# A decode-attention kernel: the feed-forward and most of the output projection in column tiles, and its code moved by a block

## The chip, the cores and the metric

The kernel runs on one core of one Trainium2 chip. The metric is the device time of one execution in microseconds (us), as the median of several runs. The profile shows one execution with the work of each engine: PE is TensorE (PEld its weight loads, issued ahead of their matmuls), DVE is VectorE, ACT is ScalarE, POOL is GpSimd, and SP is SyncE, which issues nearly all transfers here.

## What is computed

One decode step of attention over a long cache, plus a small feed-forward net, on the same normalized input (2 sequences, one new token each, width 512, 32 heads of 128, 8192 cached keys and values per head, feed-forward width 1792, all in bf16):

```python
def _A_ref(x, k_cache, v_cache, wq, wo):
    q = (x @ wq).reshape(B, Sq, H, Dh).transpose(0, 2, 1, 3)
    scores = jnp.einsum("bhqd,bhkd->bhqk", q, k_cache) * (Dh ** -0.5)
    p = softmax(scores, axis=-1)
    o = jnp.einsum("bhqk,bhkd->bhqd", p, v_cache)
    return o.transpose(0, 2, 1, 3).reshape(B, Sq, H * Dh) @ wo

def _B_ref(x, w1, w2):
    return jnp.maximum(x @ w1, 0) @ w2

xn = layernorm(x)
out = x + _A_ref(xn, k_cache, v_cache, wq, wo) + _B_ref(xn, w1, w2)
```

The caches are 134 MB each; everything else together is 12 MB.

## The kernel before, in words

**Tiling.** The 64 pairs of sequence and head are taken four at a time, in 16 steps. In a step each of the 128 partitions holds 256 keys of one pair (32 partitions per pair), so one K tile `ks` is 128 x 32768 bf16, 8.4 MB, and one V tile `vs` the same. Each exists once: a tile is loaded again only when its last reader is done.

**A step on TensorE** (the loop over `n16`). It waits for K (`dK[0]`, and `dK[1]` for the second half where a load is cut in two). Line 275 transposes 256 blocks of 128x128 into PSUM (`tp`); VectorE and ScalarE copy them to `kT` (line 429). Line 282 multiplies each by the four queries into `Sc`, the scores. VectorE takes maxima (476, 483), TensorE turns and spreads them (294, 300), ScalarE makes the exponentials `prm` (550). Line 335 multiplies the 256 blocks of V by `prm` into `ot`. Then, in all but the last two steps, line 346 issues `WARM` = 24 matmuls of 512 columns whose result nobody reads. All this is written out in code, some 1,600 instructions of a weight load and a matmul each per pair, and the loop jumps back over them.

**Transfers** are queued by SP in program order (line 182): K of the next step when the transposes of this one are done (`pT`), V of the next when line 335 is done (`sW`). The loads of steps 0 and 15 (K) and of steps 1 and 15 (V) are cut in halves. After the last transposes SP issues `w1`, `w2` and `wo` into the place of `ks` (lines 190 to 194), `wo` in four pieces cut at rows 18, 26 and 30 of 32 (`cuts`).

**Ahead of the loop**: `wq` into the place of `vs`, the layer norm on VectorE, four transposes (248), the q projection in 32 matmuls of 512 columns (254), four transposes (264). **Behind the loop** on TensorE, in its order: the softmax denominators (356, four f32 matmuls), the residual x into `fin` (362), the hidden layer (373: 14 x 4 matmuls with 128x128 weights and 2 moving columns, read from `w1` with a step of 14 elements), the transposes of the heads' outputs (385), their spreading over partitions (389), then line 400 in `project`: `w2` (14 x 4 matmuls) and the four pieces of `wo` (32 x 4), each again with 128x128 weights and 2 moving columns, all accumulated in `fin`, which is transposed with the features on the partitions. At last VectorE copies `fin` to `yT` (526), TensorE transposes it (420), VectorE copies it to `osb` (528) and SP stores it.

Of the kernel before, what the change touches and what calls it, by code (L numbers as in the profile page):

```python
# [7 lines left out]
ALU = mybir.AluOpType  # L8
ACTF = mybir.ActivationFunctionType
AX = mybir.AxisListType  # L10

U = 4
# [4 lines left out]
TR = (21, 25)  # L17
BC = 32
WARM = 24
ON_ACT = (0, 3, 5)  # L20


@with_exitstack
def kernel(
# [13 lines left out]
    P = 128  # L38
    HP = P // U
    bf16 = mybir.dt.bfloat16  # L40
    f32 = mybir.dt.float32

    Bsz, Sq, D = A_x.shape
# [3 lines left out]
    KT = D // P  # L47
    FJ = Dff // P
    KB = Sk // HP
    N = Bsz * H  # L50
    NP = N // U
    WJ = H * Dh // P
# [7 lines left out]
    QG = H * Dh // 512  # L60
    QH = 512 // Dh
    Z = (QG - 1) * Bsz

    inv_sqrt = float(Dh) ** -0.5
    eps = 1e-5
# [3 lines left out]
    def sb(shape, dt, name):  # L69
        return ctx.enter_context(nc.sbuf_tensor(name, shape, dt))  # L70
# [4 lines left out]
    def sem(name):  # L75
# [6 lines left out]
    wo_sb = ks[:, 0:WJ * D].rearrange("p (j n) -> p j n", j=WJ)  # L82
    w1_sb = ks[:, WJ * D:WJ * D + KT * Dff].rearrange("p (kt f) -> p kt f", kt=KT)
    w2_sb = ks[:, WJ * D + KT * Dff:WJ * D + KT * Dff + FJ * D].rearrange(
        "p (j n) -> p j n", j=FJ
    )
    kT = [sb([P, EG, P], bf16, f"kT{i}") for i in range(NG)]
    identb = sb([P, P], bf16, "identb")
# [8 lines left out]
    rinv = sb([Bsz, 1], f32, "rinv")  # L97
    xn = sb([Bsz, KT, P], bf16, "xn")

    xz = sb([P, KT, 2 * Z + Bsz], bf16, "xz")  # L100
    qs = sb([QG * Bsz, 512], bf16, "qs")
    qb = sb([P, N], bf16, "qb")
    q4 = sb([P, U], bf16, "q4")
# [15 lines left out]
    OG = sb([P, 2, N], f32, "OG")  # L119
    OTn = sb([P, Bsz, H], bf16, "OTn")  # L120
    Ob = sb([H, Bsz, Dh], bf16, "Ob")
    OX = sb([P, WJ, Bsz], bf16, "OX")
    hT = sb([P, FJ, Bsz], bf16, "hT")
    yT = sb([P, Bsz, KT], bf16, "yT")
    osb = sb([Bsz * KT, P], bf16, "osb")

# [25 lines left out]
    wo_v = A_wo.rearrange("(p j) n -> p j n", j=WJ)  # L152
    cuts = (0, 18, 26, 30, WJ)
    NC = len(cuts) - 1

    KSPLIT = (0, NP - 1)
    VSPLIT = (1, NP - 1)
# [4 lines left out]
    tpx = tp[0][:].rearrange("p g k -> p (g k)")[:, 0:KT * Bsz].rearrange(  # L162
        "p (kt b) -> p kt b", b=Bsz
    )
    hp = ms[:, 128:128 + FJ * Bsz].rearrange("p (j b) -> p j b", b=Bsz)
    ox = ms[:, 256:256 + Bsz * WJ]
    fin = Sc[:, 512:512 + KT * Bsz]

# [42 lines left out]
    @(lambda f: f(nc.gpsimd))  # L211
    def _(g):
        g.memset(identb[:], 0.0).then_inc(sG, 1)
        g.memset(sel[:], 0.0).then_inc(sG, 1)
        g.memset(onesh[:], 0.0).then_inc(sG, 1)
        g.wait_ge(sG, 1)
        g.affine_select(
            out=identb[:], in_=identb[:], compare_op=ALU.not_equal, fill=1.0,
            base=0, pattern=[[-1, P]], channel_multiplier=1,
        ).then_inc(sI, 1)  # L220
        g.wait_ge(sG, 2)
        g.affine_select(
            out=sel[:], in_=sel[:], compare_op=ALU.not_equal, fill=1.0,
            base=0, pattern=[[-1, DQ], [1, P]], channel_multiplier=-DQ,
        ).then_inc(sI, 1)
        g.wait_ge(sI, 2)
        g.memset(prm[:], 0.0).then_inc(sG, 1)
        g.wait_ge(sG, 4)
        for u in range(U):
            g.memset(onesh[u * HP:(u + 1) * HP, u, :], 1.0).then_inc(sI, 1)  # L230
            g.wait_ge(sI, 3 + u)
        g.wait_ge(sV, 100)
        for t in range(NP):
            if t > 0:
                g.wait_ge(sS, 2 * t)
            g.tensor_copy(q4[:], qb[:, U * t:U * t + U]).then_inc(sQ1, 1)  # L236
            for d, split in ((dK, KSPLIT), (dV, VSPLIT)):
                if t not in split:
                    g.wait_ge(d[0], 16 * (t + 1)).then_inc(d[1], 16)
        g.wait_ge(dO, 16).then_inc(sG, 1)  # L240


    @(lambda f: f(nc.tensor))
    def _(pe):
        pe.wait_ge(sI, 1)
        pe.wait_ge(sV, 5)
        for kt in range(KT):
            i = pe.transpose(tpx[:, kt, :], xn[:, kt, :], identb[0:Bsz, 0:Bsz])
        i.then_inc(sQ, 1)
        pe.wait_ge(sV, 6)  # L250
        pe.wait_ge(dQ, 16)
        for g in range(QG):
# [53 lines left out]
        with pe.Fori(16, NL + 1, 16) as n16:  # L306
            pe.wait_ge(dK[0], n16)
            for e in range(NG):
                if e == NG // 2:
                    pe.wait_ge(dK[1], n16)  # L310
                if e >= 4:
                    pe.wait_ge(kR[(e - 4) % HG], h[(e - 4) // HG])
                transposes(e)
                if e >= LAG:
                    scores(e - LAG)
            pe.wait_ge(sQ1, reg)
            for e in range(NG - LAG, NG):
                if e >= NG - 4:
                    pe.wait_ge(kR[e % HG], h[e // HG])
                scores(e)  # L320
                if e == TR[0]:
                    turn(0)
                if e == TR[1]:
                    spread(0)
            pe.wait_ge(sO, reg)
            for kk in range(KB):
                i, first = divmod(kk, KB // 2)
                if first == 0:
                    pe.wait_ge(sP, g[i])
                    if i == 0:  # L330
                        turn(1)
                    pe.wait_ge(dV[i], n16)
                if kk == BC:
                    spread(1)
                t = pe.matmul(  # L335
                    oh[:, i, :],
                    lhsT=vs[:, kk * Dh:(kk + 1) * Dh],
                    rhs=rep(prm[:, kk, :], REP),
                    start=(first == 0),
                    stop=(first == KB // 2 - 1),  # L340
                )
                if first == KB // 2 - 1:
                    t.then_inc(sW, 1)
            with pe.If_lt(reg, NP - 1):
                for i in range(WARM):
                    pe.matmul(  # L346
                        ms[:], lhsT=identb[:],
                        rhs=identb[:].rearrange("p (o k) -> p o k", o=1).to_broadcast([P, 4, P]),
                        start=True, stop=True,
                    )  # L350
            advance(pe, regs)

        pe.wait_ge(sI, 2 + U)
# [4 lines left out]
                start=True, stop=True,  # L358
            )
        t.then_inc(sH, 1)  # L360
        for k in range(KT):
            pe.matmul(
                fin[:, k * Bsz:(k + 1) * Bsz],
                lhsT=xsb[:, k * P:(k + 1) * P],
                rhs=identb[0:Bsz, 0:Bsz],
                start=(k == 0),
                stop=False,
            )
        pe.wait_ge(dW1, 16)
        w1_v = w1_sb.rearrange("p kt (f j) -> p kt j f", j=FJ)  # L370
        for j in range(FJ):
            for kt in range(KT):
                i = pe.matmul(
                    hp[:, j, :],
                    lhsT=w1_v[:, kt, j, :],
                    rhs=xz[:, kt, Z:Z + Bsz],
                    start=(kt == 0),
                    stop=(kt == KT - 1),
                )
        i.then_inc(sF, 1)  # L380

        pe.wait_ge(sV, 108)
        tO = tp[0][0:H, 0:Bsz, :]
        for b in range(Bsz):
            t = pe.transpose(tO[:, b, :], OTn[:, b, :], identb[:])
        t.then_inc(sH, 1)
        pe.wait_ge(sV, 109)
        for dq in range(DQ):
            t = pe.matmul(
# [5 lines left out]
            )  # L395
        t.then_inc(sH, 1)

        def project(w, j, x, last=False):
            for k in range(KT):
                t = pe.matmul(  # L400
                    fin[:, k * Bsz:(k + 1) * Bsz],
                    lhsT=w[:, j, k * P:(k + 1) * P],
                    rhs=x[:, j, :],
                    start=False,
                    stop=(last and k == KT - 1),
                )
            return t

        pe.wait_ge(sF, 2)
        pe.wait_ge(dW2, 16)  # L410
        for j in range(FJ):
            project(w2_sb, j, hT)
        pe.wait_ge(sV, 110)
        for c in range(NC):
            pe.wait_ge(*piece[c])
            for j in range(cuts[c], cuts[c + 1]):
                t = project(wo_sb, j, OX, j == WJ - 1)
        t.then_inc(sH, 1)
        pe.wait_ge(sV, 111)
        pe.transpose(  # L420
            tp[1][0:Bsz * KT, 0, :], yT[:].rearrange("p b c -> p (b c)"), identb[:]
        ).then_inc(sH, 1)

    def kcopies(eng, act, h):
# [8 lines left out]
    def _(v):  # L433
        v.memset(eps_t[:], eps).then_inc(sV, 1)
        v.memset(onesb[:], 1.0)
        v.memset(xz[:], 0.0).then_inc(sZ, 1)
        v.wait_ge(dX, 16)
        v.bn_stats(out=stats[:], in_=xsb[:]).then_inc(sV, 1)
        v.wait_ge(sV, 2)
# [50 lines left out]
        def both(ap):  # L490
# [21 lines left out]
        v.tensor_tensor(  # L512
            out=OTn[:].rearrange("p b h -> p (b h)"), in0=OG[:, 0, :], in1=OG[:, 1, :], op=ALU.add
        ).then_inc(sV, 1)
        v.wait_ge(sF, 1)
        v.tensor_scalar(
            out=hT[:], in0=hp, scalar1=0.0, scalar2=None, op0=ALU.max,
        ).then_inc(sF, 1)
        v.wait_ge(sH, 2)
        v.tensor_copy(Ob[:], tp[0][0:H, 0:Bsz, :]).then_inc(sV, 1)  # L520
        v.wait_ge(sH, 3)
        v.tensor_copy(
            OX[:], ox.rearrange("p (b j) -> p j b", b=Bsz)
        ).then_inc(sV, 1)
        v.wait_ge(sH, 4)
        v.tensor_copy(yT[:], fin.rearrange("p (c b) -> p b c", c=KT)).then_inc(sV, 1)
        v.wait_ge(sH, 5)
        v.tensor_copy(osb[:], tp[1][0:Bsz * KT, 0, :]).then_inc(sE, 1)


    @(lambda f: f(nc.scalar))
    def _(a):
# [29 lines left out]
            advance(a, regs)  # L562
        a.wait_ge(sV, 102)
        a.activation(out=F[:], in_=df[:], func=ACTF.Exp, scale=1.0).then_inc(sA, 1)
# [1 line left out]
_INS = ['A_x', 'A_k_cache', 'A_v_cache', 'A_wq', 'A_wo', 'B_x', 'B_w1', 'B_w2']  # L566
_OUTS = [((2, 1, 512), 'bfloat16')]
# [25 lines left out]
```

## Time and profile before

| | |
|---|---|
| median of 5 runs | 659.32 us (658.63 to 660.49) |
| the profiled execution, its own time | 659.06 us |
| its span in the profile | 657.2 us |
| busy share of the span: PE, PEld, DVE, ACT, POOL | 90%, 82%, 40%, 44%, 1% |
| moved from memory | 280.5 MB, 427 GB/s over the span |
| granted TensorE clock, mean | 0.98 |

The span is what the profile covers; 1.86 us of the execution's time lie around it. Lines of the chain give start, length, and the engine and line, or the transfer, that the time went to; "issue" is time in which the engine waited for nothing that the profile shows. Lines of the timeline give start, length, engine, line, operation and count, and in brackets the idle time ahead of it with what ended it. Matmul ends are modelled, so their starts are the better guide.

### The profile page before, as it was taken

How to read it: one execution, taken by the hardware profiler on the slowest of the kernel's cores; microseconds unless marked ns; L12 is line 12 of the kernel's file. 1: busy time of each engine (PE TensorE's matmuls, PEld its weight loads, DVE VectorE, ACT ScalarE, POOL GpSimd, SP SyncE). 2: the span in 40 equal slices, each digit the busy share in tenths (PEclk: the TensorE clock that was granted, in tenths of full speed). 3: DMA queues.
4: the chain of work that ended last, by engine and by line, in shares of the span. 5: the costliest groups of instructions: out<-in, count | busy, mean ns of one | idle time of the engine just before them, and what ended most of it. 6: DMA issues, size and time to landing. Idle time of an engine off the chain costs nothing.

```text
span 657.2 us, 27600 instructions
## 1 busy us (share of the span) xinstructions
PE 592.9 (90%) x12987; PEld 535.8 (82%) x12987; DVE 261.7 (40%) x503; ACT 290.7 (44%) x532; POOL 7.1 (1%) x30
## 2 busy tenths in 40 slices
PE   2786999999999999999989999998999999999997
PEld 0586887978878797887969888796987879698986
DVE  1440451717235071633507153260715426071721
ACT  1332543536344363634526354353735435372820
POOL 2000000000000000000000000000000000000000
PEclk9986999999999999999999999999999999999996
DMA  9999999999999999999999999999999999999996
GB/s 383 444 441 425 408 431 443 443 419 447 415 447 431 431 443 419 443 431 435 431 427 443 431 439 423 435 439 427 447 423 435 439 427 447 419 435 417 435 420 271
DMA packets 6223, 280.66 MB, mean 427 GB/s; under 512 B 706, under 2 KB 708, under 8 KB 964
## 3 DMA queue, kind: packets, MB, share of 16 engines
q1 hardware_dynamic: 6208, 280.50, 98.9%
q8 instruction: 8, 0.13, 0.1%
q14 instruction: 3, 0.02, 0.0%
q10 hardware_dynamic: 4, 0.00, 0.0%
HBM read 280.50 MB, written 0.00 MB: 427 GB/s over the span
## 4 chain that ended last, share of the span: by engine, by line
DMA 57%; PE 41%; issue 1%; DVE 0%; SPq 0%; ACT 0%; ACTq 0%
DMA ks<-in_A_k_cache_dram 53%; PE tp L275 34%; DMA ks<-in_A_wo_dram 4%; PE Sc L282 3%; PE ot L335 3%; PE ms L346 1%; DVE mcol L476 0%; ACT L429 0%; ACT kT L429 0%; PE Sc L400 0%; SPq L194 0%; PE ms L294 0%; PE ms L300 0%; SPq L191 0%; SPq L182 0%
## 5 line engine op out<-in xcount | busy, mean ns | idle before, releaser
L429 DVE COPY kT<-tp 128x1024 bf16<-128x1024 bf16 x320 | 209.2, 687 | 248.2 <-PE tp L275 242.5
L275 PEld LDWEIGHTS tp<-identb,ks 128*128 128x128 bf16 x4096 | 230.1, 98 | 26.6 <-DMA ks<-in_A_k_cache_dram 25.2
L275 PE MATMUL tp<-identb,ks 128*128 128x128 bf16 x4096 | 233.1, 220 | 19.4 <-DMA ks<-in_A_k_cache_dram 18.5
L429 ACT COPY kT<-tp 128x1024 bf16<-128x1024 bf16 x192 | 188.1, 1014 | 130.5 <-PE tp L275 130.5
L282 PE MATMUL Sc<-q,kT 128*128 128x64 bf16 (+8 forms) x4096 | 134.2, 192 | 3.2 <-issue 3.1
L282 PEld LDWEIGHTS Sc<-q,kT 128*128 128x128 bf16 x4096 | 129.6, 98 | 4.7 <-issue 3.4
L335 PE MATMUL ot<-prm,vs 128*128 128x64 bf16 x4096 | 130.6, 192 | 1.6 <-issue 1.6
L335 PEld LDWEIGHTS ot<-prm,vs 128*128 128x128 bf16 x4096 | 126.6, 97 | 3.5 <-issue 1.7
L346 PE MATMUL ms<-identb 128*128 128x512 bf16 x336 | 74.8, 379 | 0.0
L476 DVE TENSOR_REDUCE mcol<-Sc 32x1 bf16<-32x128 f32 x128 | 37.0, 289 | 93.6 <-PE Sc L282 92.3
L550 ACT ACTIVATE prm<-Sc,nm 32x128 bf16<-32x128 f32 x128 | 68.9, 538 | 5.4
L545 ACT COPY nm<-ms 128x4 f32<-128x4 f32 x32 | 5.2, 162 | 139.9 <-PE ms L300 139.9
L346 PEld LDWEIGHTS ms<-identb 128*128 128x128 bf16 x336 | 31.9, 98 | 36.4
L561 ACT COPY OTf<-ot 128x8 f32 x16 | 2.6, 165 | 69.9 <-PE ot L335 69.9
L550 ACT ACTIVATION_READ_ACCUMULATOR prm<-Sc,nm x128 | 32.0, 250 | 0.0
L294 PE MATMUL ms<-identb,mcol 128*1 128x128 bf16 x32 | 7.0, 218 | 22.1 <-DVE mcol L476 22.1
L429 ACT ACT_TABLE_LOAD x16 | 20.5, 1283 | 3.7 <-issue 3.6
L294 PEld LDWEIGHTS ms<-identb,mcol 128*1 128x1 bf16 x32 | 2.5, 79 | 23.9 <-issue 23.1
L254 PE MATMUL ot<-vs,xz 128*16 128x512 bf16 x32 | 8.5, 431 | 8.6 <-DMA vs<-in_A_wq_dram 8.6
L483 DVE TENSOR_REDUCE mx<-ms 1x4 bf16<-1x128 bf16 x32 | 8.9, 279 | 13.8 <-PE ms L294 13.8
L254 PEld LDWEIGHTS ot<-vs,xz 128*16 128x16 bf16 x32 | 3.1, 98 | 13.6 <-issue 10.7
L236 POOL COPY q<-qb 128x4 bf16<-128x4 bf16 x16 | 3.0, 186 | 590.8 <-PE Sc L282 572.5
(61 smaller groups left out, 47.6 us busy)
## 6 DMA issues: line engine op xcount, KB each, us to landing
ks<-in_A_k_cache_dram SPq DMA_DIRECT2D x4, 4096.0 KB, 23.0
vs<-in_A_v_cache_dram SPq DMA_DIRECT2D x4, 4096.0 KB, 21.8
vs<-in_A_wq_dram SPq DMA_DIRECT2D x1, 4096.0 KB, 12.1
ks<-in_B_w_dram SPq DMA_DIRECT2D x2, 1792.0 KB, 16.5
ks<-in_A_wo_dram SPq DMA_DIRECT2D x1, 2304.0 KB
ks<-in_A_wo_dram SPq DMA_DIRECT2D x1, 1024.0 KB, 26.4
ks<-in_A_wo_dram SPq DMA_DIRECT2D x1, 512.0 KB, 27.1
ks<-in_A_wo_dram SPq DMA_DIRECT2D x1, 256.0 KB, 27.3
```

What stands on the lines that cost most here:

```text
L236: g.tensor_copy(q4[:], qb[:, U * t:U * t + U]).then_inc(sQ1, 1)
L254: i = pe.matmul(qp, lhsT=xz[:, kt, Z - g * Bsz:Z - g * Bsz + QG * Bsz], rhs=vs[:, (kt * QG + g) * 512:(kt * QG + g + 1) * 512], start=(g = ...
L275: t = pe.transpose(tp[e % 4][:, i, :], ks[:, kk * Dh:(kk + 1) * Dh], identb[:])
L282: t = pe.matmul(Sc[:, U * kk:U * (kk + n)], lhsT=kT[e][:, i, :], rhs=rep(q4[:], n), start=True, stop=True,)
L294: pe.transpose(trp[:, i * P:(i + 1) * P], mcol[:, i:i + 1], identb[:]).then_inc(sT, 1)
L335: t = pe.matmul(oh[:, i, :], lhsT=vs[:, kk * Dh:(kk + 1) * Dh], rhs=rep(prm[:, kk, :], REP), start=(first == 0), stop=(first == KB // 2 - 1),)
L346: pe.matmul(ms[:], lhsT=identb[:], rhs=identb[:].rearrange("p (o k) -> p o k", o=1).to_broadcast([P, 4, P]), start=True, stop=True,)
L429: fn(kT[e][:], tp[e % 4][:]).then_inc(kR[e % HG], 1)
L476: m = v.tensor_reduce(out=mcol[own, i:i + 1], in_=S[own, i * KB // 2:(i + 1) * KB // 2, u], axis=AX.X, op=ALU.max,)
L483: v.tensor_reduce(out=mx[:, i, :], in_=trp[:, i * P:(i + 1) * P].rearrange("o (u m) -> o u m", u=U), axis=AX.X, op=ALU.max, negate=True,). ...
L545: a.copy(nm[:, i, :], bc[:, i, :]).then_inc(sN, 1)
L550: x = a.activation(out=prm[own, k, u], in_=S[own, k, u], func=ACTF.Exp, bias=nm[own, i, u:u + 1], scale=1.0, accum_out=RS[own, i, bass.ds( ...
```

## The change

The order of the transfers and the arithmetic stay. Five things change.

1. **The hidden layer** swaps its operands: the stationary operand is the input, padded with zeros to `CT` = 32 columns, and the moving one is 512 columns of `w1`. Four matmuls in turn write the four groups of 32 partitions of one PSUM bank (`tile(hp, c)`). ScalarE copies the bank to SBUF as bf16 (`hb`), TensorE transposes it (four transposes), VectorE applies the maximum into `hT`, whose unused columns GpSimd has set to zero.
2. **`w2` and pieces 0 and 1 of `wo`** are taken the same way, 14 + 18 + 8 matmuls of 512 columns, spread by `j % 4` over four groups of 32 partitions of `y`; x is added with one more. VectorE copies `y` to SBUF as f32 (`ys`), and four f32 matmuls with `sel2`, a matrix of ones and zeros that adds the four groups, bring it into `fin`. Pieces 2 and 3 stay as they were; the four f32 matmuls stand between them.
3. **51 matmuls** of 128x128 that nobody reads (`EARLY`) stand behind the first four transposes.
4. **The 24 unused matmuls** of a step become a loop of 4 times 6, and step one skips them too.
5. `sel2` is made by VectorE ahead of the layer norm; two areas are cleared by GpSimd.

```diff
+EARLY = 51
+CT = 32
+    TC = P // CT
+    QW = 512 // P
+    first_j = [min(c * QW, FJ - QW) for c in range(TC)]
+    slots = sorted({j - f + c * QW: j for c, f in enumerate(first_j) for j in range(f, f + QW)}.items())
+    slot = {j: s for s, j in slots}
...
-    OX = sb([P, WJ, Bsz], bf16, "OX")
-    hT = sb([P, FJ, Bsz], bf16, "hT")
+    hT = sb([P, P // CT * QW, CT], bf16, "hT")
+    sel2 = sb([P, Bsz], f32, "sel2")
...
+    WIDE = 2
-    hp = ms[:, 128:128 + FJ * Bsz].rearrange("p (j b) -> p j b", b=Bsz)
+    hp = tp[2][:].rearrange("p g k -> p (g k)").bitcast(f32)
+    y = tp[1][:].rearrange("p g k -> p (g k)").bitcast(f32)
+    hb = kT[0][:].rearrange("p g k -> p (g k)")[:, 0:512]
+    OX = kT[2][:].rearrange("p g k -> p (g k)").rearrange("p (j c) -> p j c", c=CT)
+    ys = kT[1][:].rearrange("p g k -> p (g k)").bitcast(f32)
...
 # GpSimd
+        g.memset(hT[:], 0.0).then_inc(sI, 1)
...
+        g.wait_ge(sS, 2 * NP)
+        g.memset(OX, 0.0).then_inc(sI, 1)
...
 # TensorE, ahead of the q projection
+        for i in range(EARLY):
+            pe.matmul(ms[:, 0:P], lhsT=identb[:], rhs=identb[:], start=True, stop=True)
         pe.wait_ge(sV, 6)
         pe.wait_ge(dQ, 16)
...
 # TensorE, at the end of a step
-            with pe.If_lt(reg, NP - 1):
-                for i in range(WARM):
-                    pe.matmul(...)
+            with pe.If_ne(reg, 1):
+                with pe.If_lt(reg, NP - 1):
+                    with pe.Fori(0, WARM // 6):
+                        for i in range(6):
+                            pe.matmul(...)
...
 # TensorE, behind the loop
-        for k in range(KT):
-            pe.matmul(fin[:, k * Bsz:(k + 1) * Bsz], lhsT=xsb[:, k * P:(k + 1) * P], ...)
+        def tile(ap, c):
+            return ap[c * CT:(c + 1) * CT, :]
         pe.wait_ge(dW1, 16)
-        for j in range(FJ):
-            for kt in range(KT):
-                i = pe.matmul(hp[:, j, :], lhsT=w1_v[:, kt, j, :], rhs=xz[:, kt, Z:Z + Bsz], ...)
+        for kt in range(KT):
+            for c in range(TC):
+                i = pe.matmul(tile(hp, c), lhsT=xz[:, kt, Z:Z + CT],
+                              rhs=w1_v[:, kt, first_j[c]:first_j[c] + QW, :], ...)
         i.then_inc(sF, 1)
+        pe.matmul(tile(y, 0), lhsT=identb[0:Bsz, 0:CT], rhs=xsb[:], start=True, stop=False)
...
+        pe.wait_ge(sF, 2)
+        for i in range(QW):
+            t = pe.transpose(tp[3][:, i, :], hb[:, i * P:(i + 1) * P], identb[:])
+        t.then_inc(sF, 1)
...
-        pe.wait_ge(sF, 2)
+        pe.wait_ge(sF, 4)
         pe.wait_ge(dW2, 16)
         for j in range(FJ):
-            project(w2_sb, j, hT)
+            c = j % TC
+            pe.matmul(tile(y, c), lhsT=hT[:, slot[j], :], rhs=w2_sb[:, j, :], start=(0 < j < TC), stop=False)
         pe.wait_ge(sV, 110)
-        for c in range(NC):
-            pe.wait_ge(*piece[c])
-            for j in range(cuts[c], cuts[c + 1]):
-                t = project(wo_sb, j, OX, j == WJ - 1)
+        for i in range(WIDE):
+            pe.wait_ge(*piece[i])
+            for j in range(cuts[i], cuts[i + 1]):
+                t = pe.matmul(tile(y, j % TC), lhsT=OX[:, j, :], rhs=wo_sb[:, j, :],
+                              start=False, stop=(j >= cuts[WIDE] - TC))
+        t.then_inc(sH, 1)
+        for i in range(WIDE, NC):
+            if i == NC - 1:
+                pe.wait_ge(sF, 5)
+                for k in range(KT):
+                    pe.matmul(fin[:, k * Bsz:(k + 1) * Bsz], lhsT=ys[:, k * P:(k + 1) * P], rhs=sel2[:], ...)
+            pe.wait_ge(*piece[i])
+            for j in range(cuts[i], cuts[i + 1]):
+                for k in range(KT):
+                    t = pe.matmul(fin[:, k * Bsz:(k + 1) * Bsz], lhsT=wo_sb[:, j, k * P:(k + 1) * P],
+                                  rhs=OX[:, j, 0:Bsz], ...)
...
 # VectorE
+        v.wait_ge(sI, 1)
+        v.tensor_reduce(out=sel2[:], in_=identb[:].rearrange("p (c r) -> p r c", c=TC)[:, 0:Bsz, :],
+                        axis=AX.X, op=ALU.add)
...
-        v.wait_ge(sF, 1)
-        v.tensor_scalar(out=hT[:], in0=hp, scalar1=0.0, scalar2=None, op0=ALU.max).then_inc(sF, 1)
         v.wait_ge(sH, 2)
         v.tensor_copy(Ob[:], tp[0][0:H, 0:Bsz, :]).then_inc(sV, 1)
+        v.wait_ge(sF, 3)
+        v.wait_ge(sI, 4 + U)
+        v.tensor_scalar(out=hT[:, :, 0:Bsz]..., in0=tp[3]..., scalar1=0.0, scalar2=None, op0=ALU.max).then_inc(sF, 1)
...
         v.wait_ge(sH, 4)
+        v.tensor_copy(ys, y).then_inc(sF, 1)
+        v.wait_ge(sH, 5)
         v.tensor_copy(yT[:], fin.rearrange("p (c b) -> p b c", c=KT)).then_inc(sV, 1)
...
 # ScalarE, at its end
+        a.wait_ge(sF, 1)
+        a.copy(hb, hp).then_inc(sF, 1)
```

## The prediction

> **What bounds the kernel now.** I read the chain of work that ended last first, because the engines' busy shares (PE 90%) say nothing about who sets the pace. Two steps of its middle:
>
> ```profile
> 111.57 14.48 PE tp L275 x256
> 126.05 0.02 issue
> 126.07 24.16 DMA ks<-in_A_k_cache_dram
> 150.23 0.05 issue
> 150.28 14.48 PE tp L275 x256
> ```
>
> A step lasts 38.71 us (150.28 - 111.57). The chain looks like TensorE and DMA taking turns, but the 24.16 us of a load are mostly waiting behind the V load ahead of it. So I read the table by stretches over the twelve steps in between (its last two columns are the busy share of the DMA engines and GB/s):
>
> ```profile
> 127.00:588.00 461.00, 430.25 (x9480) 388.23 (x9477) 188.18 (x356) 214.22 (x394) 2.24 (x12) 1.00 1.00 433
> ```
>
> The DMA engines are full. The trace's single packet records agree: a 64 KB packet takes 2.42 us on one of 16 engines, sixteen of them (one K and one V load) 38.7 us, the length of a step. From 2.0 us on no engine pauses for more than about 1 us. The kernel is a stream of 280.5 MB, with 2 us ahead of it and 4.2 us behind it (last `wo` packet 653.06, end 657.2). A change pays only if it shortens the stream, makes an engine's queue run dry, or moves what follows the last landing.
>
> Step one is where queues could run dry, so I read the chain there:
>
> ```profile
> 44.03 4.04 PE Sc L282 x127
> 48.07 0.15 PE ms L294
> 48.21 3.11 issue
> ...
> 59.25 4.88 PE ot L335 x140
> 64.13 1.59 issue
> 65.72 2.71 PE ot L335 x84
> 68.43 5.18 PE ms L346 x24
> 73.61 14.31 PE tp L275 x256
> 87.92 0.02 issue
> 87.94 23.59 DMA ks<-in_A_k_cache_dram
> ```
>
> Two stalls wait on nothing but code. They are 255 matmul pairs and two lone waits apart, 512 instructions, and the instruction queue moved eight packets of 16 KB in the whole run (29.4, 41.6, 49.0, 56.2, 63.3, 70.4, then 645.7 and 651.1):
>
> ```profile
> q8 instruction: 8, 0.13, 0.1%
> ```
>
> So code comes in blocks of 256 instructions. Behind 64 KB packets a block takes 7.3 us from entering the block ahead of it (43.97 to 51.32). After step one the loop needs none.
>
> Last, TensorE at the end (start, length, line, count, and the idle time ahead of it):
>
> ```profile
> 641.72 1.07 PE L356 MATMUL Sc<-RS,onesh 128*128 128x32 f32 x8
> 642.90 3.52 PE L373 MATMUL ms<-xz,ks 128*128 128x2 bf16 x56
> 647.44 1.66 PE L400 MATMUL Sc<-hT,ks 128*128 128x2 bf16 x56
> 649.34 2.06 PE L400 MATMUL Sc<-OX,ks 128*128 128x2 bf16 x72 [0.24 <-DMA ks<-in_A_wo_dram]
> 651.68 1.01 PE L400 MATMUL Sc<-OX,ks 128*128 128x2 bf16 x32 [0.28 <-DMA ks<-in_A_wo_dram]
> 652.92 1.00 PE L400 MATMUL Sc<-OX,ks 128*128 128x2 bf16 x24 [0.23 <-DMA ks<-in_A_wo_dram]
> ```
>
> Every `wo` piece finds TensorE waiting. The chain splits the last row: 16 matmuls at 652.92, the last eight at 653.55, done 653.94. Only those eight and the small steps behind them are not hidden.
>
> **The change, part by part.**
>
> *Small matmuls removed.* 56 (w1), 56 (w2) and 104 of 128 (wo) go, 27 ns a pair at L400 and 62 at L373. All end before the piece they wait for, so their removal is worth nothing.
>
> *Wide matmuls added.* 16 + 1 + 14 + 26 of 512 columns. No row shows matmuls in different column strips. The nearest rows stream 512 columns in 0.216 us each at full clock (L346, 24 in 5.18 us) and in 0.43 us at half clock (the first seven starts of L254). If strips overlap, four cost one: 0.054 to 0.107 us a matmul; if not, 0.216 to 0.43. I take the overlap: four neighbours write four different groups of 32 partitions from four different groups of 32 columns, and L400 shows that TensorE can issue a pair every 27 ns. For the clock I take half, since the granted clock is 0.50 in 649.0-653.5. Then w2 (14 x 0.107 = 1.5) fits between hT, about 646.1, and piece 0 at 649.34. The first 18 wo matmuls take 1.9, the next eight, from 651.68, 0.86: done 652.6 with 0.1 for the last to drain. The relu's detour (ScalarE copy about 0.55, half of L429's 1014 ns for twice the columns; four transposes at 57 ns) is hidden by the same wait for piece 0.
>
> The Trainium skill ("TensorE: Matmul & The Clock Gate", Part 3) gives 2.38x for three column tiles. By that efficiency, 0.79, the matmul would be 0.136 us and the estimate below 0.15 us later. No run here shows it. Against the change speaks "TensorEngine Tiling (Array Packing)", Key Properties: changing the tiling mode drains TensorE. It gives no time, and no row here has one.
>
> *The way back from the wide form.* VectorE copies y, 128x512 f32 out of PSUM: L458 moves 512 f32 columns in 0.68, so 652.6 + 0.05 + 0.68 = 653.35. TensorE meanwhile does piece 2's 16 matmuls (loads end 652.92 + 16 x 0.027 = 653.35). Then four f32 matmuls with 128x128 weights, which stand between piece 2 and piece 3 in TensorE's queue. L356's four calls show as eight records 0.11 us apart: 0.88. Piece 3's eight matmuls, visible at 653.53, are now queued behind them: 653.4 + 0.88 + 8 x 0.027 + 0.17 to drain = 654.65 instead of 653.94. **+0.7 us on the path**, the one certain cost. Its bounds: 0 if pieces 2 and 3 are late anyway, +1.9 if wide matmuls and copy end 1 us later.
>
> *Code.* The first stall fixes a block boundary 433 pairs into the loop, so the loop now begins about 100 instructions ahead of a boundary. 102 more put its head 2 instructions behind that boundary. The loop shrinks from about 1,600 to 1,570 instructions and ends just inside the eighth block; the block after it is fetched in step one, and the shorter tail fits it. The two late fetches leave the stream's end. In the packet records the engine that lands last (653.06) falls 0.8 us behind across the 645.7 fetch; the next ends at 652.28. Gain: 0 to 0.8. I take 0.3, as the same block's fetch in step one can delay the same engine.
>
> *Step one.* Boundaries lie 51 pairs earlier. At 7.3 us a block the stall in the scores ends near 48.7 instead of 51.3, but the clock falls as before (0.58 in 49-57) and more scores remain; the first half of ot begins about 57.7 instead of 57.3. The last seven ot pairs then lie in the next block, there at 70.4 to 72.5. The 24 unused matmuls (5.18 us) are skipped, so the transposes begin when K lands, about 72.8, instead of 73.45. But the idle wait halves the clock, as it did for the second half of the first K load (128 transposes in 8.63 us at 33.81, 7.32 at 23.33: 1.3 us for a 2.8 us cold stretch), so they need up to 2.2 us more: next K issue at 89.5 instead of 87.94. That is free until about 89.9: ten DMA engines finish V at 89.8-90.2, six at 91.3-91.7, and packets follow an issue within 1.84 us. I take +0.1.
>
> *Rolled loop.* Four branches of about 0.2 us and register adds of 0.08 issue while matmuls run; even unhidden, 1.1 us fit the 0.6 us ahead of the K landing plus 2.5 us until the last DMA engine would miss the next K.
>
> *Rest.* 51 small matmuls lie in the 8.6 us wait for wq; sel2 delays the layer norm by about 0.4 us in the same wait; the two memsets are on an idle POOL. Nothing.
>
> **Sum.** 0.7 - 0.3 + 0.1 = +0.5 us on the profiled execution's 659.06 us (span 657.2, 1.86 around it), the median being 0.26 above it: 659.32 + 0.5 = **659.8 us**, own range 658.8 to 660.8. Differences under 0.2% (1.3 us) are about what a measurement of this kernel cannot tell from none.
>
> **Rivals.**
> *Column strips run one after another* (slower). At 0.216: w1 ends 646.3, w2 begins 647.6 and ends 650.6, wo 656.2, copy 656.9, then 1.27: 658.2, +4.3, so 663.6 us; at half clock and with w1's strided reads (62 against 27 ns) up to 676. It decides above (653.4 - 0.75 - 649.34) / 26 = 0.13 us a wide matmul. For it: the only 512-column rows are serial. Against: nothing shared. 0.15.
> *Step one starves the stream* (slower). A K issue after 89.9 costs one for one; one more half-clock window of 3.4 us makes that +1.4: 661.2. 0.12.
> *The loop's head is overwritten* (slower). If it misses its boundary, every step refetches six blocks, 44 us at 7.3, more than a step: +80 us or more. The margin is 2 instructions. 0.03.
> *The stream's end gains in full* (faster). The landing comes 0.8 earlier without the late fetch, 1.4 if the late K issue also evens out the engines (their mean end is 651.6), and the f32 matmuls are done while piece 3 is awaited: 657.9 to 658.5. Against: in the queue they follow piece 2. 0.20.
> *Forecast*: 0.50.
>
> Faster by over 0.2% (below 658.0) takes half of the gain case, since medians scatter by some tenths (five runs: 658.63 to 660.49), and the forecast's lower edge: 0.12. Slower (above 660.6) takes the strips, two thirds of the starved case, the overwritten head and the forecast's upper edge: 0.31. The rest, 0.57, lies within. The range 658.0 to 663.6 leaves out about 0.1 on each side.
>
> **What would show it.** Right: steps of 38.7 us; no instruction fetch between 100 and 650 us; wide starts that average under 0.13 us; eight f32 records between pieces 2 and 3, and the last small matmul near 654.6 less what the landing gained. Wrong: wide starts 0.2 us apart, a gap ahead of the third K load, fetches inside later steps, or a last matmul earlier than 653.9.

## The result, and the profile after

The changed kernel takes **661.36 us** (median of 33 runs, 659.37 to 665.55) against 659.66 us for the kernel before (59 runs, 658.24 to 661.98): ratio **1.0028, 95% interval [1.002, 1.0036]**, slower by about 1.8 us. The profile shows an execution of 662.98 us (span 660.3), which is 1.6 us above its own median; its times are read here for where they go, and the medians for how much. Steps are counted from one here and below: step one is the first round of the loop.

The chain of waits of the changed kernel, in step two (line 293 is now the transposes, 275 before):

```profile
41.19 31.61 DMA ks<-in_A_k_cache_dram
72.80 0.05 issue
72.84 16.32 PE tp L293 x256
89.16 0.02 issue
89.18 24.20 DMA ks<-in_A_k_cache_dram
113.38 0.05 issue
113.42 14.48 PE tp L293 x256
```

Transposes that took 14.31 us take 16.32, and the third K load is issued at 89.18 instead of 87.94. The next transposes begin 1.85 us later than before (113.42 - 111.57), and the lag does not shrink again: 2.03 us one step on, 2.6 from the step after that, 2.67 at step 15, 2.5 when the second last piece of `wo` is seen.

The table by stretches of the changed kernel (its last three columns are the granted clock, the busy share of the DMA engines, and GB/s):

```profile
69.92:76.74 6.82, 4.45 (x44) 4.30 (x45) 1.38 (x2) 2.73 (x4) 0.00 (x0) 0.50 0.91 387
72.84:89.20 16.36, 16.36 (x263) 16.36 (x264) 12.33 (x19) 11.73 (x12) 0.00 (x0) 0.88 1.03 444
127.00:588.00 461.00, 429.45 (x9480) 387.40 (x9478) 187.43 (x355) 213.02 (x394) 2.24 (x12) 1.00 1.00 432
```

The first row says why the transposes are longer: the clock was 0.50 from 69.92 to 76.74, where the kernel before had 1.00:

```profile
69.92:76.74 6.82, 6.82 (x77) 4.85 (x75) 1.98 (x3) 2.65 (x4) 0.00 (x0) 1.00 0.94 401
```

The last row says that the long middle is as full as it was.

TensorE's timeline in step one of the changed kernel:

```profile
46.70 1.71 PE L300 MATMUL Sc<-q,kT 128*128 128x8 bf16 x50 [1.71 <-issue]
53.73 0.27 PE L300 MATMUL Sc<-q,kT 128*128 128x16 bf16 x4 [2.56 <-issue]
63.47 4.02 PE L353 MATMUL ot<-prm,vs 128*128 128x64 bf16 x128 [2.18 <-issue]
70.33 0.56 PE L353 MATMUL ot<-prm,vs 128*128 128x64 bf16 x7 [2.83 <-issue]
72.84 1.46 PE L293 MATMUL tp<-identb,ks 128*128 128x128 bf16 x12 [1.96 <-DMA ks<-in_A_k_cache_dram]
```

Four stalls for code, 9.3 us in sum, where there were two (4.7 us). The last is followed by seven pairs and by 1.96 us of waiting for K.

The page's row of the instruction queue (packets, MB, share):

```profile
q8 instruction: 7, 0.11, 0.1%
```

Seven fetches instead of eight; in the trace's records the last begins at 74.34, and none follows to the end of the span. TensorE's timeline at the end of the changed kernel:

```profile
645.92 1.07 PE L376 MATMUL Sc<-RS,onesh 128*128 128x32 f32 x8
646.92 3.82 PE L388 MATMUL tp<-ks,xz 128*32 128x512 bf16 x16
651.42 0.40 PE L407 MATMUL tp<-identb,kT 128*128 128x128 bf16 x4 [0.16 <-ACT kT L617]
652.10 1.04 PE L424 MATMUL tp<-ks,hT 128*32 128x512 bf16 x14
652.76 2.02 PE L432 MATMUL tp<-ks,kT 128*32 128x512 bf16 x26
655.41 0.55 PE L451 MATMUL Sc<-kT,ks 128*128 128x2 bf16 x16 [0.63 <-DMA ks<-in_A_wo_dram]
655.83 1.03 PE L441 MATMUL Sc<-sel,kT 128*128 128x2 f32 x8
656.72 0.34 PE L451 MATMUL Sc<-kT,ks 128*128 128x2 bf16 x8
```

From piece 2 seen to the last matmul done it is now 1.66 us (655.41 to 657.07); before it was 1.02 (652.92 to 653.94). The eight f32 records stand between pieces 2 and 3.

### The profile page after: what moved, and what is told of

Same layout as the page of the kernel before. It is cut to its first block, busy times and chain, and to the rows that moved or that the text cites. A ratio compares the mean times of both kernels' runs of the same rounds, so it can differ in the third digit from the quotient of the medians.

```text
span 660.3 us, 27489 instructions
## 1 busy us (share of the span) xinstructions
PE 594.3 (90%) x12863; PEld 533.7 (81%) x12863; DVE 262.6 (40%) x505; ACT 291.4 (44%) x533; POOL 8.6 (1%) x32
## 4 chain that ended last, share of the span: by engine, by line
DMA 61%; PE 37%; SPq 0%; ACT 0%; issue 0%; DVE 0%; ACTq 0%
DMA ks<-in_A_k_cache_dram 57%; PE tp L293 34%; DMA ks<-in_A_wo_dram 4%; PE Sc L300 1%; PE ot L353 1%; ACT L469 0%; DVE mcol L522 0%; ACT kT L469 0%; PE Sc L441 0%; SPq L207 0%; PE Sc L451 0%; SPq L204 0%; SPq L195 0%; SPq L183 0%; PE ms L312 0%
## 5 line engine op out<-in xcount | busy, mean ns | idle before, releaser
L353 PE MATMUL ot<-prm,vs 128*128 128x64 bf16 x4096 | 132.7, 193 | 5.0 <-issue 5.0
L300 PE MATMUL Sc<-q,kT 128*128 128x64 bf16 (+8 forms) x4096 | 132.8, 191 | 4.3 <-issue 4.3
L353 PEld LDWEIGHTS ot<-prm,vs 128*128 128x128 bf16 x4096 | 128.6, 98 | 7.0 <-issue 5.2
L300 PEld LDWEIGHTS Sc<-q,kT 128*128 128x128 bf16 x4096 | 128.2, 97 | 5.8 <-issue 4.5
L601 ACT ACTIVATE prm<-Sc,nm 32x128 bf16<-32x128 f32 x128 | 68.9, 539 | 5.4
L366 PE MATMUL ms<-identb 128*128 128x512 bf16 x312 | 69.4, 379 | 0.0
L366 PEld LDWEIGHTS ms<-identb 128*128 128x128 bf16 x312 | 29.6, 98 | 33.8
```

The source lines that it names most:

```text
L300: t = pe.matmul(Sc[:, U * kk:U * (kk + n)], lhsT=kT[e][:, i, :], rhs=rep(q4[:], n), start=True, stop=True,)
L353: t = pe.matmul(oh[:, i, :], lhsT=vs[:, kk * Dh:(kk + 1) * Dh], rhs=rep(prm[:, kk, :], REP), start=(first == 0), stop=(first == KB // 2 - 1),)
L366: pe.matmul(ms[:], lhsT=identb[:], rhs=identb[:].rearrange("p (o k) -> p o k", o=1).to_broadcast([P, 4, P]), start=True, stop=True,)
L601: x = a.activation(out=prm[own, k, u], in_=S[own, k, u], func=ACTF.Exp, bias=nm[own, i, u:u + 1], scale=1.0, accum_out=RS[own, i, bass.ds( ...
```

## The experiments

Theory at the outset: most of the loss arises in step one and two, by unused matmuls that are skipped (a cold clock, a late K issue), and the tail costs about what was predicted. Rival: the tail, or the moved code itself, costs it. Each kernel ran beside the kernel before on the same chip, in five rounds.

### The tail alone

The changed kernel with `EARLY = 0` and the unused matmuls back in step one:

```diff
-    EARLY = 51
+    EARLY = 0
-            with pe.If_ne(reg, 1):
-                with pe.If_lt(reg, NP - 1):
+            with pe.If_lt(reg, NP - 1):
```

> The changed kernel without the 51 extra matmuls and with the 24 unused matmuls in step one as well (still rolled), so that step one is laid out as before and only the new tail and the rolled loop are left. Theory A (the time goes in step one: the third K load is asked for too late and the DMA engines run dry): steps run on the grid of the kernel before, third K load landed near 111.5 us instead of 113.4, and only the f32 matmuls between pieces 2 and 3 remain, +0.6 us, so a median 0.5 to 0.8 us above the kernel before. Theory B (the tail costs it all): +1.5 to 2 us, as in the full change.

Measured: 660.44 us, ratio 1.0006 [0.9988, 1.0025]. Step one is as before (transposes at 73.71 for 14.31 us, K issue 88.03, next transposes 111.65). Its chain of waits at the end:

```profile
650.53 1.53 PE tp L431 x26
652.06 0.02 issue
652.08 0.70 DVE kT L574
652.78 0.04 issue
652.83 1.05 PE Sc L440 x8
653.88 0.21 PE Sc L450 x8
```

The ratio's centre is 0.4 us, the +0.7 - 0.3 of the prediction, but its interval holds zero. The chain adds something: no load stands in it. The last packet lands at 652.30, 0.76 earlier than in the kernel before, and the landing no longer matters: from the wide matmuls through VectorE's copy to the f32 matmuls, TensorE's own order sets the end (654.09 against 653.94). One of the two late fetches is missing in this profile; what that may have given is eaten by the new tail itself.

### Step one alone

The kernel before with the 51 matmuls, the rolled loop and the skip, and its old tail:

```diff
+        for i in range(51):
+            pe.matmul(ms[:, 0:P], lhsT=identb[:], rhs=identb[:], start=True, stop=True)
         pe.wait_ge(sV, 6)
...
+            with pe.If_ne(reg, 1):
+                ... (the rolled loop of the change)
```

> The kernel before with the 51 extra matmuls, the rolled loop and its skipping in step one, but its old tail. Theory A: third K load landed near 113.4 us, +1.2 us or a little more in the median (the whole change less the f32 matmuls). Theory B: no change, within 0.3 us. Rival C (the code fetches at the end of the stream matter): its longer code fetches blocks in the tail as well, which would add up to 0.8 us at the last landing beside A's loss.

Measured: 662.21 us, ratio 1.0026 [1.0012, 1.004]. The transposes of step two take 16.11 us from 72.98, the third K load is issued at 89.11 and takes 24.73, the next transposes begin at 113.88. The ratio is that of the whole change, but not all of it comes from step one: with the long tail the moved boundary falls between its last pieces, and its chain of waits shows a stall there that neither kernel has:

```profile
655.04 0.27 PE Sc L404 x4
655.31 1.67 issue
656.98 0.71 PE Sc L404 x20
```

### Six of the 24 unused matmuls kept in step one

```diff
+            with pe.If_lt(reg, NP - 1):
+                for i in range(6):
+                    pe.matmul(ms[:], lhsT=identb[:], ...)
-            with pe.If_ne(reg, 1):
-                with pe.If_lt(reg, NP - 1):
-                    with pe.Fori(0, WARM // 6):
+                with pe.If_ne(reg, 1):
+                    with pe.Fori(0, WARM // 6 - 1):
```

> The changed kernel, with 6 of the 24 unused matmuls kept in step one (18 are skipped there). Theory A with the clock as its first cause: these 6 bridge the wait from 70.9 to 72.8 us, the clock is full again by about 73.5, the 256 transposes take 14.5 us instead of 16.3, the third K load is asked for near 88 us, and most of 1.2 us comes back. If the clock isn't the cause, or the 6 at half clock (0.43 us each, 2.6 us) delay the transposes by as much as they save: no change, or up to 1 us worse.

Measured: 660.01 us, ratio 0.9999 [0.9983, 1.0015]. Three lines of its chain of waits:

```profile
70.68 2.50 PE ms L364 x6
73.18 14.78 PE tp L293 x256
...
112.41 1.62 PE tp L293 x29
```

Six matmuls fill the wait, the transposes need 14.78 us instead of 16.32, the next begin 1.0 us earlier than in the changed kernel, and the loss is gone, with the code still moved: the interval lies below that of the changed kernel. (The six lengthen the code, and one fetch is back at the end, at 653.90.) The bridge over the wait was what the skip took away. TensorE would have been ready earlier still, near 111.0, but the granted clock was 0.50 once more from 97.93 to 101.34, and 256 matmuls of `ot` took 9.33 us instead of 7.94.

### The skip without the moved code

```diff
-    EARLY = 51
+    EARLY = 0
```

> The changed kernel without the 51 extra matmuls: the blocks of code lie as before, step one still skips the unused matmuls. It asks which of the two edits of step one does the harm. If the shift of the code (stalls at other places, the last seven ot matmuls behind a block of their own): step one ends near 68.4 us again and the third K load lands near 111.6. If the skipping (the clock halves while TensorE waits from 68.4 to 72.8 us): the transposes take 15.5 to 16.3 us, the third K load is asked for at 88.5 to 89.2 us and lands 0.5 to 2 us late; then the median stays 1 us or more above the kernel before.

Measured: 661.40 us, ratio 1.0025 [1.001, 1.004]. TensorE's timeline in step one:

```profile
66.10 2.71 PE L353 MATMUL ot<-prm,vs 128*128 128x64 bf16 x84 [1.54 <-issue]
72.84 1.46 PE L293 MATMUL tp<-identb,ks 128*128 128x128 bf16 x12 [4.04 <-DMA ks<-in_A_k_cache_dram]
```

And the row of its table by stretches that follows the wait (third from the end: the granted clock):

```profile
72.76:76.17 3.41, 3.33 (x32) 3.33 (x33) 1.24 (x2) 1.01 (x1) 0.00 (x0) 0.50 1.05 452
```

Here TensorE is done with V at 68.9, waits 4.04 us for K, and gets half a clock for the first 3.41 us. In the chain of waits:

```profile
72.84 16.04 PE tp L293 x256
...
99.89 8.35 PE ot L353 x224
108.24 5.18 PE ms L366 x24
113.42 0.61 PE tp L293 x11
```

The transposes need 16.04 us, and the next begin at 113.42, as late as in the changed kernel. With the new tail in both, skipping without the moved code costs as much as the whole change. The kernel with the tail alone differs by the skip only; its ratio is 1.0006, though the two intervals overlap.

No load stands between 72.84 and 113.42 in this chain: it is TensorE that is late, a point to which the cut load below comes back. But 1.48 us of its lateness has another source: the granted clock was 0.50 a second time, from 100.06 to 103.48, and the 224 matmuls of `ot` took 8.35 us instead of 6.87. Without that window TensorE would have been ready at 111.94, and the K load, whose last packet ends at 112.27, would have set the next start.

### The moved code with every unused matmul in place

```diff
-            with pe.If_ne(reg, 1):
-                with pe.If_lt(reg, NP - 1):
+            with pe.If_lt(reg, NP - 1):
```

> The changed kernel with all 24 unused matmuls in step one too, rolled; the 51 extra matmuls stay. The matmuls then begin only near 71 us, at half clock first, and end near 78 us: if the order of arrival is what counts (theory A), the transposes begin 5 us late, the third K load is asked for near 92.5 us, lands near 115 to 117, and the median is 3 to 6 us above the kernel before. If keeping the clock full is worth more than the delay: no worse than the changed kernel.

Measured: 663.90 us, ratio 1.006 [1.0039, 1.008], the slowest of all. From its chain of waits:

```profile
69.79 3.10 issue
72.89 0.56 PE ot L353 x7
73.45 7.91 PE ms L365 x24
81.36 14.29 PE tp L293 x256
```

The moved boundaries end V's part of step one 5.0 us later than in the kernel before (68.43 to 73.45), and the unused matmuls, which take 7.91 us instead of 5.18, end at 81.36. This execution took 667.59 us, 3.7 us above the median, so its times are on the high side; in the changed kernel's profile the same part of V ends near 70.9. Still, moving the code is not free: it has to be paid for by leaving unused matmuls out. The change leaves out all of them, six kept are better, all kept are far too many.

This execution shows its fetches at 46.5, 54.1, 63.3 and 70.5; the changed kernel's has them at 44.2, 51.3, 60.9 and 68.1. The next experiment, whose TensorE code is that of the changed kernel, has them at 46.7, 53.9, 63.2 and 70.8. The same code thus fetched in two phases, 2.3 to 2.7 us apart, about one 64 KB packet (2.42). That may be why single runs of the changed kernel lie up to 6 us apart; it was not tested.

### The third K load cut in two

If the loss comes through a K load that is issued too late, issuing its first half earlier should take it away.

```diff
-    KSPLIT = (0, NP - 1)
+    KSPLIT = (0, 2, NP - 1)
```

In the changed kernel:

> The changed kernel with one edit: the third K load is cut in two halves, the first of which is asked for when half of the transposes of step one's successor are done, about 7 us earlier. Code and clock of TensorE in step one stay as they are. Theory A: the DMA engines never run dry, the third K load has landed by 111.5 to 112 us, and the median falls by 1.2 to 1.9 us, to 0.3 to 0.7 above the kernel before. If the loss came from stalls for code or from the half clock by themselves, it stays at +1.5 to 2.

Measured: 660.73 us, ratio 1.0006 [0.9989, 1.0022]. Its profile fell in the later phase of the fetches, so its trace cannot be laid beside that of the changed kernel. So the same cut was made in the kernel with the skip but without the moved code, and in the kernel before:

> The changed kernel without the 51 small matmuls (the code where it was) and with the third K load cut in two halves; step one still skips the unused matmuls. Without the cut this kernel took 661.40 us (ratio 1.0025 [1.001, 1.004]), its transposes of step two began at 72.84 and lasted 15.82 us, and the next transposes began at 113.25 instead of 111.57. Theory (what the slow clock costs comes only through the third K load, which is issued too late for the queues): the transposes stay at 15.5 to 16.3 us, the first half of the load is issued near 81, no engine begins a packet late, the next transposes begin at 111.5 to 112.5, and the time falls to 659.6-660.6, ratio 0.999 to 1.0015. Rival (the loss is in the step's slow TensorE work or in the tail, whatever the queue does): it stays at 661.0-661.8, ratio 1.002 or more.

> The kernel before with only the third K load cut in two halves: what the cut does by itself. Theory: the third K load of the kernel before is issued at 87.94, and only the engines with slack run dry; the cut gains nothing that the end sees, ratio 0.999 to 1.001 (659.2-660.3). Rival (the cut is a gain of its own, so that the recovery of a changed kernel by it says nothing about the late issue): ratio below 0.998, under 658.5. The cut could also cost, if two loads of half the size move slower: above 1.001.

Measured: the first 660.55 us, ratio 1.0014 [1.0, 1.0027], against 1.0025 [1.001, 1.004] without the cut; the kernel before with the cut 660.18 us, ratio 1.0006 [0.9991, 1.0021]. The time falls by about half of the loss and the intervals overlap, so the times settle nothing. The chain of the first does:

```profile
72.83 17.25 PE tp L293 x256
...
107.95 5.18 PE ms L366 x24
113.13 14.31 PE tp L293 x256
```

The load is out of the chain, as the theory had it: all engines go from V into K without a pause. But the next transposes hardly begin sooner, at 113.13, because **TensorE itself is late**. Its own work from one start of transposes to the next is 37.35 us at full clock (112.38 - 75.03, in the kernel before with the cut, where nothing stands between). In the kernel before that leaves 0.6 us of slack (73.61 + 37.35 = 110.96, K seen at 111.57). With 17.25 us of transposes instead of 14.29 it ends at 72.83 + 37.35 + 2.96 = 113.14; the trace shows 113.13. The rival of this experiment, that the loss is TensorE's own slow work, was right for this half: two paths run side by side, the K load and TensorE, and the cold window makes both late.

### Cheaper partial sums

The copy of `y` and `sel2` in bf16, which rounds the partial sums; the four f32 matmuls become bf16 ones:

```diff
-    sel2 = sb([P, Bsz], f32, "sel2")
+    sel2 = sb([P, Bsz], bf16, "sel2")
-    ys = kT[1][:].rearrange("p g k -> p (g k)").bitcast(f32)
+    ys = kT[1][:].rearrange("p g k -> p (g k)")[:, 0:512]
...
-            axis=AX.X, op=ALU.add,
+            axis=AX.X, op=ALU.max,
```

(`sel2` is now made with a maximum instead of a sum; at most one element of each group is not zero, so it stays the same.)

With the six matmuls kept:

> The kernel with 6 unused matmuls in step one, and y copied to SBUF as bf16 with a bf16 sel2, so that the four matmuls between pieces 2 and 3 run in bf16 (they round the four partial sums to bf16). If the f32 form is the price of the tail (eight records 0.11 us apart): the four matmuls show as four records about 0.03 us apart, 0.75 us less behind the last landing, so 0.5 to 0.9 us below the kernel before. If the price lay in the copy of y or the order of the queue: no change against the run with 6 matmuls.

Measured: 660.81 us, ratio 1.0009 [0.9992, 1.0025]. The four matmuls shrink to 0.10 us (from 0.90), as expected, but the time does not fall: this profile fell in the later phase (transposes of step two at 75.91, every engine dry ahead of the third K load). Inconclusive. With step one as before instead:

> The new tail alone (no extra matmuls, unused matmuls in every step), with the four matmuls between pieces 2 and 3 in bf16. By the same reckoning 0.75 us less than with f32: 0.2 to 0.6 us below the kernel before, a little above the version with the shifted code if the one late fetch of code still delays an engine at the end of the stream.

Measured: 659.03 us, ratio 0.9989 [0.9977, 1.0001]. The end of its chain of waits:

```profile
626.10 26.88 DMA ks<-in_A_wo_dram
652.99 0.05 issue
653.03 0.36 PE Sc L450 x8
```

The landing of the last piece bounds the end again, at 652.99, and 0.36 us of matmuls follow. This has the lowest median of all; its interval just reaches no change.

## Why the prediction was right or wrong

The forecast was 659.8 us with 658.0 to 663.6; measured 661.36. The range holds it, the likeliest case (658.8 to 660.8) does not, and the range does so partly by luck: its upper end was set by the rival of the column strips, which fell. The rival "step one starves the stream", at 661.2, names what happened, and I had given it 0.12; but it asked for an issue after 89.9 and one more half-clock window, and the stream starved with an issue at 89.18. That its figure fits is luck too.

**What failed is the step-one term, +0.1, by two of its steps.** The skip itself was read rightly: transposes at 72.84 (predicted 72.8), up to 2.2 us longer (measured 2.0), K issue 89.18 (predicted 89.5).

The first wrong step is "free until about 89.9". I took it from the fastest restart, 1.84 us from issue to packet, and from a count in which six engines finish V late. The same packet records of the kernel before show slower ones: two engines that had finished V by 90.2 began K at 90.32 and 90.72, 2.4 and 2.8 us after its issue, with first packets of 3.87 and 3.38 us. In the packet records of the changed kernel nine engines had finished V at 89.92 to 90.30 and stood still until 90.21 to 91.19, 1.0 to 2.0 us after the issue; the first packet of eight of them then took 2.8 to 3.4 us instead of 2.42. They end K at 111.56 at the latest, where the last engine of the kernel before ended at 111.09. The other seven finished V at 91.35 to 91.78. Six of them went on without a pause; one, which finished at 91.52, began K only at 92.28, 3.1 us after the issue, and its first packet took 3.81 us. (The records name no engine; this is the one end of V that no packet follows at once.) That is 0.76 + 1.39 = 2.15 us lost, and it ends K at 113.00. That a queue was full at 91.7 in the kernel before said nothing about what an issue 1.24 us later does to an engine that comes by then. Why this one engine of seven stopped stays open. The later lag seems to come the same way: near 169 us five first packets of a K load take 3.4 to 4.5 us.

The second wrong step is one that is missing. I weighed the longer transposes against the queue alone and used TensorE's 0.6 us of slack only for the rolled loop. By 72.84 + 37.35 + 2.0 TensorE could not have begun before 112.2 even with the load in time: +0.6 us that no early issue would have saved. In the changed kernel it then waits 1.22 us for K:

```profile
113.42 2.74 PE L293 MATMUL tp<-identb,ks 128*128 128x128 bf16 x46 [1.22 <-DMA ks<-in_A_k_cache_dram]
```

The kernel with the skip and the cut load shows this path alone.

**The tail** was right in size and partly in mechanism. The way back costs +0.64 us in the profile (predicted +0.7); the copy of `y` took 0.69 us (predicted 0.68), the f32 matmuls 0.89 (0.88). The copy was hidden behind piece 2's matmuls; the f32 matmuls in TensorE's queue are the cost. From the start of step 15's transposes to the landing of piece 2 the trace shows 76.71 us instead of 76.89, and 76.03 in the kernel with the tail alone, which has one late fetch less: by these single profiles a late fetch was worth 0.2 to 0.9 us (predicted 0.3). The tail alone measured +0.4 in its ratio, with an interval that also holds zero.

**The column strips overlap**, so the rival "one after another" falls. The starts of the wide matmuls at L424 and L432 come in groups of four within 10 ns, a group every 0.215 us: 0.054 us a matmul. The Trainium skill's 2.38x for three strips ("TensorE: Matmul & The Clock Gate", Part 3) is less than that; here four strips measured as four. (The prediction's sentence on that figure is mis-added: by its own terms the estimate would be about 0.3 us later, not 0.15. Likewise its bound of +1.9 us for a copy 1 us later comes to +1.7. Neither is a term of the sum.) Between 128-column and 32-column matmuls no pause of the drain ("TensorEngine Tiling (Array Packing)", Key Properties) stands out of the records: the first of L388 starts 0.21 us after the last of L376, whose own records stand 0.11 us apart. The half clock that I took for the wide matmuls did not come either: the granted clock was 1.00 from 646.9 to 657.0, and 0.107 us became 0.054.

**Wrong, and hidden: the hidden layer.** By the prediction's 0.107 us a matmul its 16 wide matmuls take 1.7 us; they take 3.82, at full clock. Their moving operand is read from `w1` with a step of 14 elements, and a group of four starts every 0.90 us; the step is the one difference that stands out, though no run changed it alone. So `w2` began at 652.10, and the matmuls of piece 0 at 652.76, 1.9 us after it landed (650.90); by piece 1 TensorE waited again. The strided reads that I had charged to the strips' rival cost every version of the change. In the kernel with the tail alone they are part of the chain that sets the end.

**The code** lies where predicted: the stalls come after 126 score pairs, ahead of the last four, after 121 pairs of ot (32 and 89) and ahead of the last seven; the head is not overwritten, since no fetch falls into the later steps. In time the first stall in the scores came earlier: it ended at 46.70 instead of near 48.7; in the later phase it ends at 49.01 (the kernel with every unused matmul).

## What to carry to other kernels

An unused stretch of work ahead of a wait may be holding up two things: the clock for what follows, and the time at which the next transfer is issued; before it is removed, keep the few matmuls that reach to the end of the wait. When a step gets longer, hold it against every path that closes in that step, the transfer's queue and the engine's own next start, and take for the transfer the slowest engine's restart, not the fastest. Moving code by a block to spare a fetch at the end puts stalls elsewhere; count them all, and what must be left out to pay for them.

## What the runs showed of the hardware

- A transfer that meets empty queues starts unevenly: nine of 16 engines began 1.0 to 2.0 us after the issue, one 3.1, and the first packet took up to 3.81 us (near 169 us up to 4.47) instead of 2.42. Six of the seven engines that were done with the load ahead 2.2 us or more after the issue went on without a pause.
- Four strips of 32 columns run fully beside each other: 0.215 us for four matmuls of 512 columns, the 0.216 us of a single full one.
- Four strips whose moving operand has a step of 14 bf16 elements took 4.2 times as long as those with a contiguous one: 0.90 us against 0.215 for a group of four.
- The half clock after a wait is paid in the next step: 256 transposes that need 14.3 us took 16.04 to 17.25 where TensorE had idled 2 to 4 us ahead of them, and 14.78 where six matmuls filled that wait.
- Single stretches of 3.41 us at half clock also fall inside the long middle, in six of the twelve profiles. Two of them made the matmuls of `ot` in their step 1.39 and 1.48 us longer.
